# Reordering VectorE work in the opening of a fused attention and MLP kernel, with four softmax normalizations moved to GpSimd

## The chip, the core and the metric

The kernel runs on one core of a Trainium2 chip. The metric is the device time of one execution in microseconds. Engines are named as in the profile: PE is TensorE (matmul), PEld its weight loads, DVE is VectorE, ACT is ScalarE, POOL is GpSimd, SP is SyncE, which here only issues DMAs.

## The reference

Chunked attention, then two MLPs, all in float32 (the weights arrive as float64):

```python
scores = scale * np.matmul(q_c, k_c.transpose(0, 1, 2, 4, 3))     # chunks of 64
scores = scores - np.max(scores, axis=-1, keepdims=True)
attn = np.exp(scores)
attn = attn / (np.sum(attn, axis=-1, keepdims=True) + 1e-09)
out = np.matmul(attn, v_c)
...
h = x @ w_in                       # x: 2304 x 512, w_in: 512 x 2048
g = h * (1.0 / (1.0 + np.exp(-h)))
x = (g @ w_out)
...
a = x @ w_a                        # 512 x 1536
b = x @ w_b
return (a * b @ w_out).astype(np.float32)
```

## The kernel before

The 2304 tokens are 18 tiles of 128. A matrix product in full precision is made of three products of high and low parts: an operand is split by ACT, which writes a rounded high part, and by DVE, which subtracts it to leave the low part. That holds for the attention output (xhi, xlo), the activations (ghi, glo) and the weights (wA).

A weight tile of 128 x 512 passes six stations. SP fetches the float64 words into one of three slots of raws (`fetch`). ACT scales the upper words (`scaled`, L147). DVE makes the magnitude in two operations (`magnitude`, L155 and L158), then puts in sign and lower mantissa bits in two more (`begin`, L174 and L178). ACT rounds the high part (`upper`, L196). DVE subtracts for the low part (`lower`, L203). `weights` advances several tiles by one station in one call, and is called twice in each step of the first MLP. Tiles 0 and 1 of the weights are w_in[0] and w_out[0], tiles 2 and 3 w_in[1] and w_out[1], and so on; 32 of them pass L196 and L203.

The opening is written out by hand (source lines 816 to 902): it takes token tiles 0 to 5 through attention and mixes in the first weight tiles. For tile i, `S(i)` is the scores on PE (L253), `att_max` the row maximum and its subtraction on DVE (L267 to L272), `att_exp` the exponential on ACT, `att_norm` the sum, a reciprocal (L302) and a product with it (L303) on DVE, `Tr(i)` a transposition on PE (L312), `rest["P", i]` its copy out of PSUM by ACT (L316), `V(i)` the product with the values on PE (L335), `rest["X", i]` its high part by ACT (L347) and `rest["L", i]` its low part by DVE (L351). `V(4)` is written into the PSUM bank with the tag sA. `busy(n)` (L705) issues n idle matmuls on zeros, also into bank sA; each is two rows of the trace. Token tiles 0 to 3 are the first block of the MLP, tiles 4 and 5 a side block.

`front_a` is a product of the first MLP into bank mm or at (L370), followed on ACT by two sigmoid-gated activations (g at L399, ghi at L400) and on DVE by the low part glo (L396); `back` is the second product (L418). After the opening a loop over steps k follows: the next front product, the side block's back product, `weights`, the side block's front product, `weights`, the back product. Each engine takes its instructions in the order of the program; a PSUM bank or buffer that is reused makes its new writer wait for the last reader of the old contents.

Of the kernel before, what the change touches and what calls it, by code (L numbers as in the profile page):

```python
# [22 lines left out]
def chunk_attention_silu_mlp_gated_mlp(  # L23
# [35 lines left out]
    nc = tc.nc  # L59
# [43 lines left out]
    def bank(tag, shape):  # L103
        return psum.tile(shape, F32, tag=tag, name="ps_" + tag)

    def slot(name, dt=F32R):
        return big.tile([P, 4 * DM], dt, tag="b", name=name)
# [19 lines left out]
    def fetch(src, dest):  # L127
        raw = raws[:, turn[0] % RAWS]
        turn[0] += 1
        nc.sync.dma_start(out=raw, in_=src)  # L130
        fetched.append((dest, raw))

    def leave(n=0):

        while len(leaving) > n:
            dst, src = leaving.pop(0)
            nc.sync.dma_start(out=dst, in_=src)

    def words(raw):
        w32 = raw.bitcast(U32).rearrange("p (f t) -> p f t", t=2)  # L140
        return w32[:, :, 0], w32[:, :, 1]

    def scaled():

        dest, raw = fetched.pop(0)
        w = spool.tile([P, DM], F32, tag="tmp", name="w", bufs=3)
        nc.scalar.activation(w, words(raw)[1].bitcast(F32), AF.Copy, scale=2.0**111)  # L147
        opened.append((dest, raw, w))

    def magnitude():  # L150

        if not opened:
            return
        w = opened[0][2]
        nc.vector.tensor_scalar(  # L155
            out=w, in0=w, scalar1=2.0**-126, scalar2=2.0**-97, op0=ALU.mult, op1=ALU.mult
        )
        nc.vector.tensor_scalar(  # L158
            out=w.bitcast(U32),
            in0=w.bitcast(U32),  # L160
            scalar1=3,
            scalar2=0x7FFFFFFF,
            op0=ALU.logical_shift_left,
            op1=ALU.bitwise_and,
        )

    def begin():

        if not opened:
            return  # L170
        dest, raw, w = opened.pop(0)
        low, high = words(raw)
        wu = w.bitcast(U32)
        nc.vector.scalar_tensor_tensor(  # L174
            out=wu, in0=high, scalar=0x80000000, in1=wu,
            op0=ALU.bitwise_and, op1=ALU.bitwise_or,
        )
        nc.vector.scalar_tensor_tensor(  # L178
            out=wu, in0=low, scalar=29, in1=wu,
            op0=ALU.logical_shift_right, op1=ALU.bitwise_or,  # L180
        )
        if dest[0] == "f":
            wf[dest[1:]] = d = dram.tile([P, DM], F32, name=f"wf{dest[1]}{dest[2]}")
            leaving.append((d, w))
        else:
            stage_1.append((dest, w))

    def upper():
        if not stage_1:
            return  # L190
        dest, w = stage_1.pop()
        _, m, j = dest
        if m not in slots_a:
            slots_a[m] = slot("wA").rearrange("p (j n) -> p j n", j=4)
        hl = slots_a[m][:, 2 * j:2 * j + 2]
        nc.scalar.activation(hl[:, 0], w, AF.Copy)  # L196
        stage_2.append((dest, hl, w))

    def lower():
        if not stage_2:  # L200
            return
        dest, hl, w = stage_2.pop()
        nc.vector.tensor_tensor(out=hl[:, 1], in0=w, in1=hl[:, 0].bitcast(F32), op=ALU.subtract)  # L203
        wA.setdefault(dest[1], {})[dest[2]] = hl[:, 0], hl[:, 1]

    def weights(src, dest):

        leave()
        fetch(src, dest)
        upper()  # L210
        magnitude()
        begin()
        lower()
        scaled()


# [79 lines left out]
    def att_norm(i):  # L296
        s, mx, sm, rs, banks = soft[i]
        sg = s.rearrange("p h g k -> p g h k")
        if not banks:
            nc.vector.tensor_reduce(out=sm, in_=sg, op=ALU.add, axis=AX.X)  # L300
        nc.vector.tensor_scalar_add(sm, sm, EPS)
        nc.vector.reciprocal(out=rs, in_=sm)  # L302
        nc.vector.tensor_tensor(  # L303
            out=sg, in0=sg, in1=rs.unsqueeze(3).to_broadcast([P, 2, KT, 64]), op=ALU.mult
        )
        soft[i] = s

    def att_transpose(i, ptag, where, later=False):
        s = soft.pop(i).rearrange("p h g k -> p h (g k)")
        ps = bank(ptag, [P, KT, P])  # L310
        for hp in range(KT):
            nc.tensor.transpose(ps[:, hp, :], s[:, hp, :], ident)  # L312
        prob[i] = att_tile(where, "pt", i).rearrange("p (h n) -> p h n", h=KT)

        def evacuate():
            nc.scalar.activation(prob[i], ps, AF.Copy)  # L316

        if later:
            return evacuate
        evacuate()  # L320

    def att_values(i, ptags, x, o, later=False, beside=None):
        w = P // len(ptags)
        if beside is None:
            banks = [bank(t, [P, KT, w]) for t in ptags]
        else:
            banks = [t[:, 1 - r] for r, t in enumerate(soft[beside])]
        va = vs.pop(i).rearrange("p (a h d) -> p a h d", a=2, h=KT)
        half = [slice(0, 64), slice(64, 128)]
        for hp in range(KT):  # L330
            for a in range(2):
                for r in range(2):

                    ps, part, n = (banks[0], r, half[a]) if len(banks) == 1 else (banks[r], a, half[0])
                    nc.tensor.matmul(  # L335
                        ps[half[part], hp, n],
                        lhsT=va[half[r], a, hp, :],
                        rhs=prob[i][half[r], hp, half[a]],
                        start=True,
                        stop=True,  # L340
                    )
        parts = [[a[:, :, o + w * j:o + w * j + w] for a in x] for j in range(len(banks))]
        del prob[i]

        def upper():
            for ps, (hi, _) in zip(banks, parts):
                nc.scalar.activation(hi, ps, AF.Copy)  # L347

        def lower():
            for ps, (hi, lo) in zip(banks, parts):  # L350
                nc.vector.tensor_tensor(out=lo, in0=ps, in1=hi.bitcast(F32), op=ALU.subtract)  # L351

        if later:
            return upper, lower
        upper()
        lower()
# [288 lines left out]
    def next_a():  # L645
        m, j = units_a[done[0]]
        done[0] += 1
        return (w_in, w_out)[j][m], ("a", m, j)

    def prep_a():  # L650
        if done[0] < len(units_a):
            weights(*next_a())
            return True
        return False
# [8 lines left out]
    def prep_b():  # L663
        if done[1] < len(units_b):
            dest = units_b[done[1]]
            src = (w_a, w_b, w_o2)[dest[1]][dest[2]]
            weights(src, dest)
            done[1] += 1
            return True
        return False  # L670
# [11 lines left out]
    with tc.manual_schedule():  # L682
# [18 lines left out]
        def busy(n):  # L701

            ps = bank("sA", [P, P])
            for _ in range(n):
                nc.tensor.matmul(ps, lhsT=zero, rhs=zero, start=True, stop=True)  # L705

        def half(i):
            if blocks[0][1] > i:
                return x_t[0], i * P
            return x_t[SIDE], (i - blocks[0][1]) * P  # L710
# [9 lines left out]
        def v_in(*tiles):  # L720
            for i in tiles:
                load_v(i, W, nc.sync)
# [12 lines left out]
        qk_in(5)  # L735
        v_in(4)
        v_in(5)


        side_bank = {-1: "at", 0: "at", 1: "at"}  # L740

# [45 lines left out]
        def back(k):  # L787
            b, m = steps[k]
            back_a(b, m, pend.pop(k))
# [9 lines left out]
        def finish(g, k):  # L799
            if k in g:  # L800
                g[k][2]()
# [3 lines left out]
        rest = {}  # L805
# [4 lines left out]
        def Tr(i, tag):  # L810
            rest["P", i] = att_transpose(i, tag, W, later=True)

        def V(i, tag):
            rest["X", i], rest["L", i] = att_values(i, (tag,), *half(i), later=True)
# [10 lines left out]
        att_exp(1)  # L825
        magnitude()
        att_norm(0)
        busy(3)
        Tr(0, "at")
# [20 lines left out]
        rest["X", 1]()  # L850
        att_max(4, W, True)
        begin()
        fetch(*next_a())
        Tr(3, "sA")
        rest["P", 3]()
        rest["L", 1]()
# [22 lines left out]
        rest["X", 4]()  # L879
        pend[0], silu = front_a(main[0], 0, "mm", gpool, True)  # L880
        upper()
        Tr(5, "at")
        rest["L", 4]()
        lower()
        silu()
        rest["P", 5]()
        scaled()
        busy(2)
        V(5, "mm")
        finish(pend, 0)  # L890
        magnitude()
        begin()
        busy(2)
        back(0)
        rest["X", 5]()
# [430 lines left out]
```

## Time and profile before

| | |
|---|---|
| median of 3 runs | 863.2 us (862.88 to 863.54) |
| the profiled execution | 862.69 us, its span 860.9 us |
| PE busy | 846.5 us, 98% of the span |
| DVE busy | 566.7 us, 66% |
| ACT busy | 398.5 us, 46% |
| POOL busy | 50.2 us, 6% |
| PE in 0 to 30 us / 30 to 50 us | 24.14 us / 18.03 us busy |
| PE in 200 to 300 us | 100.00 of 100 us busy |
| granted TensorE clock, mean | 0.999 |

The span is the profiled time from the first to the last instruction; 1.8 us of the execution lie outside it. PE is the engine to watch: where it is busy throughout, other engines' work costs nothing; where it stands idle, the row of its next instruction says in brackets for how long and for whom.

### The profile page before, as it was taken

The page shows a single profiled execution, that of the slowest core. Times are in us where ns is not written, and L with a number is a line of the kernel's source. Part 1 is how long each engine was busy: PE and PEld are TensorE (multiplying, and loading weights), DVE is VectorE, ACT ScalarE, POOL GpSimd, SP SyncE. Part 2 cuts the span into 40 slices and gives each one's busy share as a digit, 9 for nine tenths or more (in the row PEclk, how much of TensorE's full clock was granted, in tenths as well). Part 3 has the DMA queues.
Part 4 walks back from the last instruction along what each step waited for, and adds up shares of the span by engine and source line. Part 5 has one row for each costly group of instructions (what it writes and reads, how often), then busy time and mean ns, then how long its engine had stood idle before and what let it go on. Part 6 is the DMA issues. An engine that isn't in the chain of part 4 may idle for free.

```text
span 860.9 us, 14124 instructions
## 1 busy us (share of the span) xinstructions
PE 846.5 (98%) x5474; PEld 769.5 (89%) x5474; DVE 566.7 (66%) x1029; ACT 398.5 (46%) x769; POOL 50.2 (6%) x91
## 2 busy tenths in 40 slices
PE   7999999999999999999999999999999999999998
PEld 7788888888888888888889999999999999999998
DVE  6886877855567755757865997584454594454563
ACT  5645546535454455434545554463333373333252
POOL 0000000010010100023201110000000000000000
PEclk9999999999999999999999999999999999999999
DMA  8354353337455654467799887878666888666761
GB/s 294 100 174 132 123 161 121 100 118 238 147 174 172 217 165 169 152 226 269 265 343 372 314 296 309 306 297 294 256 249 254 306 313 265 245 252 252 288 226 56
DMA packets 54034, 193.85 MB, mean 225 GB/s; under 512 B 5904, under 2 KB 13584, under 8 KB 45520
## 3 DMA queue, kind: packets, MB, share of 16 engines
q1 hardware_dynamic: 46752, 169.76, 55.5%
q0 software_dynamic: 6928, 22.81, 8.0%
q8 instruction: 43, 0.70, 0.3%
q10 hardware_dynamic: 288, 0.39, 0.1%
q14 instruction: 23, 0.19, 0.1%
HBM read 141.03 MB, written 51.90 MB: 224 GB/s over the span
## 4 chain that ended last, share of the span: by engine, by line
PE 86%; issue 5%; ACT 3%; DMA 3%; DVE 3%; POOL 0%; POOLq 0%; ACTq 0%; DVEq 0%
PE ps_acc L972 19%; PE ps_acc L418 19%; PE ps_mm L370 15%; PE ps_sA L370 7%; PE ps_at L972 5%; PE ps_sA L972 5%; PE ps_sB L972 4%; PE ps_mm L972 4%; DMA raws<-wf 2%; PE ps_sA L418 1%; PE ps_sB L418 1%; PE ps_at L370 1%; PE ps_at L253 1%; PE ps_at L335 1%; PE ps_sA L705 1%
## 5 line engine op out<-in xcount | busy, mean ns | idle before, releaser
L972 PE MATMUL ps_acc<-xo,ring 128*128 128x384 f32 x868 | 168.2, 334 | 0.6 <-DVE gq L1047 0.6
L418 PE MATMUL ps_acc<-ghi,wA 128*128 128x512 f32 x512 | 159.2, 392 | 0.0
L972 PEld LDWEIGHTS ps_acc<-xo,ring 128*128 128x128 f32 x868 | 152.1, 188 | 1.1 <-DVE gq L1047 1.1
L418 PEld LDWEIGHTS ps_acc<-ghi,wA 128*128 128x128 f32 x512 | 94.2, 188 | 19.1
L370 PE MATMUL ps_mm<-xhi,wA 128*128 128x512 f32 (+1 forms) x400 | 101.3, 375 | 3.2 <-ACT wA L196 3.2
L418 PE MATMUL ps_acc<-glo,wA 128*128 128x512 f32 x256 | 99.9, 390 | 0.0
L370 PEld LDWEIGHTS ps_mm<-xhi,wA 128*128 128x128 f32 x400 | 70.2, 188 | 17.3 <-ACT wA L196 5.1
L399 ACT ACTIVATE g<-ps_mm 128x512 f32<-128x512 f32 (+1 forms) x50 | 28.0, 559 | 102.5 <-PE ps_mm L370 96.3
L396 DVE TENSOR_TENSOR glo<-g,ghi 128x512 fp32r<-128x512 f32 x80 | 50.7, 633 | 27.2 <-ACT ghi L400 27.0
L418 PEld LDWEIGHTS ps_acc<-glo,wA 128*128 128x128 f32 x256 | 48.1, 188 | 10.2
L1107 DVE TENSOR_TENSOR u<-gq,u 128x384 fp32r<-128x384 f32 x84 | 44.5, 553 | 17.4 <-ACT u L1106 16.9
L1106 ACT ACTIVATE u<-gq 128x384 fp32r<-128x384 f32 x84 | 40.6, 516 | 30.5 <-DVE gq L1047 28.6
L972 PE MATMUL ps_acc<-u,ring 128*128 128x384 f32 x272 | 53.6, 337 | 0.3
L147 ACT ACTIVATE w<-raws 128x512 f32<-128x512 f32 x68 | 45.5, 670 | 16.6 <-DMA raws<-w_b 8.8
L370 PE MATMUL ps_mm<-xlo,wA 128*128 128x512 f32 (+1 forms) x200 | 49.9, 371 | 0.6 <-DVE xlo L351 0.6
L370 PE MATMUL ps_sA<-xhi,wA 128*128 128x512 f32 x184 | 49.6, 391 | 0.0
L972 PEld LDWEIGHTS ps_acc<-u,ring 128*128 128x128 f32 x272 | 47.6, 188 | 1.3 <-ACT gq L981 0.9
L178 DVE SCALAR_TENSOR_TENSOR w<-raws,w 128x512 uint32<-128x512 uint32 x68 | 47.1, 692 | 2.3
L174 DVE SCALAR_TENSOR_TENSOR w<-raws,w 128x512 uint32<-128x512 uint32 x68 | 47.1, 692 | 2.3
L972 PE MATMUL ps_at<-xo,ring 128*128 128x384 f32 x231 | 47.8, 334 | 0.0
L972 PE MATMUL ps_sB<-xo,ring 128*128 128x384 f32 x220 | 44.9, 334 | 0.0
L972 PE MATMUL ps_sA<-xo,ring 128*128 128x384 f32 x213 | 44.4, 335 | 0.1
(183 smaller groups left out, 1413.5 us busy)
## 6 DMA issues: line engine op xcount, KB each, us to landing
ring<-w SPq DMA_DIRECT2D x30, 1024.0 KB, 7.3
ring<-wg SPq DMA_DIRECT2D x24, 1024.0 KB, 5.1
ring<-wg SPq DMA_DIRECT2D x24, 768.0 KB, 6.3
wg<-ring SPq DMA_DIRECT2D x12, 1024.0 KB, 6.6
wf<-w SPq DMA_DIRECT2D x36, 256.0 KB, 2.2
wg<-ring SPq DMA_DIRECT2D x12, 768.0 KB, 6.5
raws<-w_in SPq DMA_DIRECT2D x16, 512.0 KB, 3.5
raws<-w_out SPq DMA_DIRECT2D x16, 512.0 KB, 3.5
```

The lines of the kernel that those rows point to most:

```text
L147: nc.scalar.activation(w, words(raw)[1].bitcast(F32), AF.Copy, scale=2.0**111)
L174: nc.vector.scalar_tensor_tensor(out=wu, in0=high, scalar=0x80000000, in1=wu, op0=ALU.bitwise_and, op1=ALU.bitwise_or,)
L178: nc.vector.scalar_tensor_tensor(out=wu, in0=low, scalar=29, in1=wu, op0=ALU.logical_shift_right, op1=ALU.bitwise_or,)
L253: nc.tensor.matmul(soft[i][j % len(soft[i])][n, j, hp, :], lhsT=q[r, hp, n], rhs=k[r, hp, n], start=True, stop=True,)
L335: nc.tensor.matmul(ps[half[part], hp, n], lhsT=va[half[r], a, hp, :], rhs=prob[i][half[r], hp, half[a]], start=True, stop=True,)
L370: nc.tensor.matmul(ps, lhsT=a[:, kk * P:(kk + 1) * P], rhs=b[:, kk, :], start=(j == 0 and kk == 0), stop=(j == 2 and kk == KT - 1),)
L396: nc.vector.tensor_tensor(out=glo, in0=g, in1=ghi.bitcast(F32), op=ALU.subtract)
L399: nc.scalar.activation(g, ps, AF.Silu)
L418: nc.tensor.matmul(acc_t[b][j], lhsT=a[:, j * P:(j + 1) * P], rhs=g, start=(m == 0 and i == 0 and (b != SIDE or j % 2 == 0)), stop=(m == M ...
L972: nc.tensor.matmul(ps, lhsT=a, rhs=b, start=first and i == 0, stop=last and i == 2, skip_group_check=True,)
L1106: nc.scalar.activation(hi, src, AF.Copy)
L1107: nc.vector.tensor_tensor(out=lo, in0=src, in1=hi.bitcast(F32), op=ALU.subtract)
```

## The change

There are four edits. In `weights`, `lower` moves ahead of `begin`. The fetch of weight tile 2 is written earlier. The L303 products of token tiles 2 to 5 go to GpSimd. Near the end of the opening, `scaled` and `magnitude` of weight tile 2 move up, and `rest["L", 4]`, the low part of token tile 4, moves down behind `begin`.

```diff
@@ weights
         upper()
         magnitude()
+        lower()
         begin()
-        lower()
         scaled()
@@ att_norm
-        nc.vector.tensor_tensor(
+        (nc.gpsimd if 1 < i < 6 else nc.vector).tensor_tensor(
             out=sg, in0=sg, in1=rs.unsqueeze(3).to_broadcast([P, 2, KT, 64]), op=ALU.mult
         )
@@ opening
         v_in(5)
-
+        fetch(*next_a())
...
         att_max(4, W, True)
         begin()
-        fetch(*next_a())
         Tr(3, "sA")
@@ opening
         pend[0], silu = front_a(main[0], 0, "mm", gpool, True)
         upper()
+        scaled()
         Tr(5, "at")
-        rest["L", 4]()
         lower()
         silu()
         rest["P", 5]()
-        scaled()
         busy(2)
         V(5, "mm")
+        magnitude()
         finish(pend, 0)
-        magnitude()
         begin()
+        rest["L", 4]()
         busy(2)
         back(0)
```

SP's rows and their order are the same in both kernels. DVE at the end of the opening, from the sum of token tile 5 on, before (`start` holds the probabilities, `ps_sA` is tile 4, `ps_mm` tile 5):

```order
L300 TENSOR_REDUCE sm<-start 128x8
L301 TENSOR_SCALAR sm<-sm 128x8
L302 RECIPROCAL rs<-sm 128x8
L303 TENSOR_TENSOR start<-start,rs 128x2x4x64
L351 TENSOR_TENSOR xlo<-ps_sA,xhi 128x4x128
L203 TENSOR_TENSOR wA<-w,wA 128x512
L396 TENSOR_TENSOR glo<-g,ghi 128x512
L155 TENSOR_SCALAR w<-w 128x512
L158 TENSOR_SCALAR w<-w 128x512
L174 SCALAR_TENSOR_TENSOR w<-raws,w 128x512
L178 SCALAR_TENSOR_TENSOR w<-raws,w 128x512
L351 TENSOR_TENSOR xlo<-ps_mm,xhi 128x4x128
```

and in the changed kernel:

```order
L300 TENSOR_REDUCE sm<-start 128x8
L301 TENSOR_SCALAR sm<-sm 128x8
L302 RECIPROCAL rs<-sm 128x8
L203 TENSOR_TENSOR wA<-w,wA 128x512
L155 TENSOR_SCALAR w<-w 128x512
L158 TENSOR_SCALAR w<-w 128x512
L396 TENSOR_TENSOR glo<-g,ghi 128x512
L174 SCALAR_TENSOR_TENSOR w<-raws,w 128x512
L178 SCALAR_TENSOR_TENSOR w<-raws,w 128x512
L351 TENSOR_TENSOR xlo<-ps_sA,xhi 128x4x128
L351 TENSOR_TENSOR xlo<-ps_mm,xhi 128x4x128
L203 TENSOR_TENSOR wA<-w,wA 128x512
```

The L303 row is gone from DVE, and the L351 row that reads ps_sA has moved behind L396, L174 and L178.

PE over the same stretch, with the semaphores that a row waits for, in the changed kernel (the rows are the first MLP product, Tr(5), busy(2) and V(5)):

```order
L370 MATMUL ps_mm<-xlo,wA 128x512 [waits DVE_49]
L370 MATMUL ps_mm<-xlo,wA 128x512 x3
L370 MATMUL ps_mm<-xhi,wA 128x512 x4
L312 MATMUL ps_at<-ident,start 128x128 [waits PE_49,Pool_49]
L312 MATMUL ps_at<-ident,start 128x128 x3
L705 MATMUL ps_sA<-start 128x128 [waits DVE_49]
L705 MATMUL ps_sA<-start 128x128
L335 MATMUL ps_mm<-start 64x64 [waits DMAHW3_49,Activation_49]
L335 MATMUL ps_mm<-start 64x64 x15
```

PE's rows stand in the same order as before; the transposition's wait has gone from DVE and ACT to POOL, and busy's first row waits for DVE in both kernels, since it writes the bank that the L351 row on ps_sA reads.

DVE in one call of `weights` in the loop and the glo behind it, before:

```order
L155 TENSOR_SCALAR w<-w 128x512
L158 TENSOR_SCALAR w<-w 128x512
L174 SCALAR_TENSOR_TENSOR w<-raws,w 128x512
L178 SCALAR_TENSOR_TENSOR w<-raws,w 128x512
L203 TENSOR_TENSOR wA<-w,wA 128x512
L396 TENSOR_TENSOR glo<-g,ghi 128x512
```

and in the changed kernel:

```order
L155 TENSOR_SCALAR w<-w 128x512
L158 TENSOR_SCALAR w<-w 128x512
L203 TENSOR_TENSOR wA<-w,wA 128x512
L174 SCALAR_TENSOR_TENSOR w<-raws,w 128x512
L178 SCALAR_TENSOR_TENSOR w<-raws,w 128x512
L396 TENSOR_TENSOR glo<-g,ghi 128x512
```

L203 now stands between the magnitude and the sign, in 27 calls.

## Rows read from the trace of the kernel before

**Rows 1.** Waits of PE over the span: us in total, times, longest
```profile
PE ps_mm L370 <- ACT wA L196: 3.2, 5, 1.3
```

**Rows 2.** PE in order of time: start, us, work, idle before
```profile
17.54 0.63 PE L312 MATMUL ps_sB<-ident,start 128*128 128x128 f32 x4 [0.52 <-DVE start L303]
...
29.01 1.20 PE L370 MATMUL ps_mm<-xlo,wA 128*128 128x512 f32 x4 [0.59 <-DVE xlo L351]
30.04 1.08 PE L370 MATMUL ps_mm<-xhi,wA 128*128 128x512 f32 x4
...
31.40 0.69 PE L705 MATMUL ps_sA<-start 128*128 128x128 f32 x4
32.79 1.15 PE L335 MATMUL ps_mm<-start 64*64 64x64 f32 x32 [0.70 <-ACT start L316]
33.87 0.71 PE L705 MATMUL ps_sA<-start 128*128 128x128 f32 x4
34.33 0.71 PE L418 MATMUL ps_acc<-ghi,wA 128*128 128x512 f32 x2
```

**Rows 3.** DVE in order of time, same stretch
```profile
16.70 0.69 DVE L303 TENSOR_TENSOR start<-start,rs 128x512 f32<-128x512 f32 x1
...
30.64 0.68 DVE L351 TENSOR_TENSOR xlo<-ps_sA,xhi 128x512 fp32r<-128x512 f32 x1
...
32.28 0.69 DVE L396 TENSOR_TENSOR glo<-g,ghi 128x512 fp32r<-128x512 f32 x1 [0.36 <-ACT ghi L400]
...
34.25 0.69 DVE L174 SCALAR_TENSOR_TENSOR w<-raws,w 128x512 uint32<-128x512 uint32 x1
34.97 0.69 DVE L178 SCALAR_TENSOR_TENSOR w<-raws,w 128x512 uint32<-128x512 uint32 x1
35.58 0.68 DVE L351 TENSOR_TENSOR xlo<-ps_mm,xhi 128x512 fp32r<-128x512 f32 x1
```

**Rows 4.** ACT in order of time, same stretch
```profile
28.54 1.28 ACT L399 ACT_TABLE_LOAD   x1
31.16 0.60 ACT L399 ACTIVATE g<-ps_mm 128x512 f32<-128x512 f32 x1 [1.34 <-PE ps_mm L370]
31.65 0.59 ACT L400 ACTIVATE ghi<-ps_mm 128x512 fp32r<-128x512 f32 x1
...
32.61 0.68 ACT L147 ACTIVATE w<-raws 128x512 f32<-128x512 f32 x1
```

**Rows 5.** POOL in order of time, its largest operation before the loop
```profile
1.02 0.29 POOL masks.py:199 TENSOR_SCALAR_AFFINE_SELECT ident<-ident 128x128 f32<-128x128 f32 x1
```

**Rows 6.** ACT, DVE, ACT and PE in order of time, first loop steps
```profile
42.60 0.63 ACT L196 ACTIVATE wA<-w 128x512 fp32r<-128x512 f32 x1
...
43.27 0.69 DVE L203 TENSOR_TENSOR wA<-w,wA 128x512 fp32r<-128x512 f32 x1 [1.09 <-ACT wA L196]
...
44.99 0.63 ACT L196 ACTIVATE wA<-w 128x512 fp32r<-128x512 f32 x1
...
45.68 1.20 PE L370 MATMUL ps_mm<-xhi,wA 128*128 128x512 f32 x4 [1.27 <-ACT wA L196]
```

**Rows 7.** DVE and ACT in order of time, softmax inside the loop
```profile
69.19 0.69 DVE L272 TENSOR_TENSOR s<-ps_at,mx 128x512 f32<-128x512 f32 x1
...
71.87 0.63 ACT L283 ACTIVATE s<-s 128x512 f32<-128x512 f32 x1
```

**Rows 8.** Busy us of PE, PEld, DVE, ACT, POOL in late stretches; PE clock
```profile
857.00:857.50 0.50, 0.33 (x2) 0.01 (x1) 0.00 (x0) 0.13 (x1) 0.00 (x0) 1.00 0.00 0
...
859.50:860.00 0.50, 0.00 (x0) 0.00 (x0) 0.00 (x0) 0.00 (x0) 0.00 (x0) 0.54 0.00 0
```

**Rows 9.** L705 in 0 to 7 and 7 to 40 us: ns min/median/max, starts
```profile
L705 PE MATMUL ps_sA<-start x24: 307/421/580, 1.1 to 6.2; 128*128 128x128 f32 x24
...
L705 PE MATMUL ps_sA<-start x38: 275/275/377, 7.5 to 34.3; 128*128 128x128 f32 x38
```

**Rows 10.** SP in order of time: the fetch of weight tile 2
```profile
13.91 0.33 SPq L130 DMA_DIRECT2D raws<-w_in  x1
```

## The prediction

> **What bounds the kernel now.** I read the busy times first, then PE's waits over the whole span, then PE, DVE and ACT in order of time through the opening. PE is busy almost throughout, so only what moves PE counts. Behind the opening PE's only repeated wait is for the high part of a weight tile, five times, 3.2 us in all [rows 1]. The opening is different: there PE stops for the others at every stage. It waits 0.52 us for a normalization before a transposition, 0.59 us for a low part inside the first product, and 0.70 us for a copy before V(5) at 32.79 [rows 2]. From V(5) on it works through to the wait before 45.68 [rows 2, 6]. So I ask one question of the opening: when does V(5) start? And one of the loop: does the wait before 45.68 grow?
>
> **The dear step: the moved low part of token tile 4.** Before, busy(2) starts at 31.40, just after DVE's subtraction on ps_sA ends (30.64 + 0.68 = 31.32) [rows 2, 3]. That is no accident: its first matmul overwrites the bank that the subtraction reads, and the rows of PE's order show it waiting for DVE in both kernels. The diff puts that subtraction behind glo, L174 and L178, but busy(2) stays where it is, ahead of V(5). PE takes its work in order, so V(5) and all behind it now wait for this chain:
>
> - the product's last four matmuls start at 30.04 and end at 31.12; g starts at 31.16, ghi 0.49 later, and ghi ends at 32.24; glo starts at 32.28 [rows 2 to 4];
> - glo lets the next DVE operation start 0.61 later (as L178 does L351, 34.97 to 35.58), L174 to L178 takes 0.72, L178 to L351 0.61 [rows 3]: the subtraction runs from 34.22 to 34.90;
> - busy(2) follows 0.08 later, as before, at 34.98, and what is behind it 0.46 after that (33.87 to 34.33) [rows 2]: V(5) at 35.44.
>
> Before it was 32.79, so this costs 2.65 us, if the product ends when it did. The copy for V(5) (0.6 us on ACT behind ghi) is long done. No work of PE's own fills the gap.
>
> **Normalization on GpSimd.** No tensor product on POOL is in the trace. Its nearest row is the affine select, 0.29 us for 128 columns [rows 5]; four times that for 512 columns is 1.16 us, which I take. Lower bound: DVE's own 0.69 us [rows 3]. Upper bound: 2.32 us, twice 1.16, for the second input. From DVE's L303 at 16.70 to the transposition at 17.54 are 0.84 us: 0.69 of work and 0.15 of handing over [rows 2, 3]. On POOL I add 0.08 us for the handing over from DVE, so the transposition slips by D + 0.15 + 0.08 - 0.84 = D - 0.61, or 0.55 us. The scores of tile 4 stand behind it on PE, DVE's maxima of tile 4 wait for them, and tile 4's own normalization adds another 0.55. Both slips reach the exponential's successors on ACT: 1.10 us at the table load. The table load ends at 29.82 and g starts at 31.16, a cover of 1.34 [rows 4]. The moved L147 takes 0.57 of that cover (0.68 less the 0.11 by which ACT's operations overlap, 31.16 to 31.65 against 0.60) [rows 4]. So g starts 1.10 + 0.57 - 1.34 = 0.33 us later, and the chain above with it. DVE's relief (0.61 us for each L303 it loses) is eaten by the first slip. With D = 0.69 the slips are nearly nothing and the relief remains: -0.53. With D = 2.32 the term is 3.42 + 0.57 - 1.34 = 2.65. Tile 5's product on POOL is hidden behind the long wait at busy(2).
>
> [...]
>
> **The low part ahead of the sign.** L203 needs ACT's L196 of the same call, and `begin` used to run while ACT got there. Now `begin` of the next tile stands behind that wait. At the first loop steps it matters: L196 of tile 3 runs from 42.60 to 43.23, L203 follows at 43.27 [rows 6]. Then L174 at 43.88 and L178 at 44.60, ending at 45.29; L196 of tile 4, which had run at 44.99, starts at 45.33. PE's product waits for exactly that [rows 6]: 0.34 us. Bounds: 0, if DVE catches up, and 0.34. Elsewhere there is room. The tightest other place that I found is the softmax inside the loop: its subtraction ends at 69.88; behind two more operations (0.72 + 0.61) it ends at 71.21, and the exponential starts at 71.87 in any case, behind its table load [rows 7]. That cover, 0.66 us, would have to go before four such places cost anything. The earlier L203 gains nothing, since PE's waits are for high parts [rows 1].
>
> **The fetch** is nothing: SP's order is unchanged, and the third tile was fetched at 13.91 already, long before ACT scales it [rows 10].
>
> **The clock.** Waiting in this way leaves PE silent from about 32.0, when Tr(5), some 0.6 us behind the product, is done, to 35.3: 3.3 us. The end of the trace shows what silence can do: PE's last work is in the half microsecond from 857.0, and in the one from 859.5 the granted clock has fallen from 1.00 to a mean of 0.54, on its way to the lower level, 1.2 GHz [rows 8]. So I expect a fall. Its price I take from the start: 24 rows of L705 took from 1.1 to past 6.2 us, some 0.22 each, at a median of 421 ns, against 275 ns later [rows 9] and 0.115 each from 33.87 to 34.33 [rows 2]. That stretch lost 24 x 0.1 = 2.4 us, my upper bound; the lower is 0. I take 1.4, somewhat over the middle, since long matmuls follow V(5). The Trainium skill (TensorE: Matmul & The Clock Gate, Part 1) states that idleness takes the clock to 1.2 GHz and work brings it back; by that the fall comes, and the traces so far bear it out at both ends.
>
> **The sum**: 2.65 + 0.33 + 0.34 + 1.4 = 4.7 us. On the profiled execution, 862.69 us (1.8 of it outside the span, untouched), that is 867.4; the median of the runs shown lies 0.5 higher, so 867.9 us.
>
> **The rivals.**
>
> 1. The wait comes, the clock stays up: 863.2 + 3.3 = 866.5 us. For it: an idle stretch of 1.27 us left the clock alone [rows 6]. Against: this one is longer than that at the end. It decides below the chosen sum, still slower.
> 2. GpSimd is the slow one, at or beyond the upper bound of 2.32: 2.65 + 2.65 + 0.34 + 1.4 = 7.0, or 870.2 us. For it: two inputs and a first use. Against: the affine select is no slower per column than half of that.
> 3. Not slower: busy(2)'s wait on DVE is met by an earlier operation than the moved subtraction. Then V(5) moves by the 0.33 of ACT alone and the loop by 0.34: 863.9 us. Against it: the start of busy(2) 0.08 us after that subtraction [rows 2, 3]. It decides if the wait is over by 32.5.
> 4. Faster: as 3, and the earlier weight work also ends all five waits for high parts: 863.9 - 3.2 = 860.7 us [rows 1]. Against it: the one before 45.68 ends with an L196 that stands behind ACT's activations, not behind DVE [rows 6].
>
> **How the numbers follow.** 0.62 for the wait with the fall of the clock, 0.23 for rival 1, 0.08 for rival 2, 0.05 for rival 3, 0.02 for rival 4. The wait with its bounds reaches from 2.65 - 0.53 = 2.1 us (no fall, cheap GpSimd, loop free) to past 6.5 (2.65 + 0.33 + 0.34 + 2.4 = 5.7, and 0.8 more for a GpSimd product of 1.56). The range is 865.4 to 869.8. It leaves out rivals 2 to 4 and the far tail. Within 0.2%, 1.7 us, a measurement of this kernel can hardly be told from no change: slower 0.92, the same 0.05, faster 0.03.
>
> **What would show it.** In the changed trace busy(2)'s row should carry an idle time of about 3 us put down to DVE's subtraction on ps_sA, with V(5) near 35.8, and the granted clock should dip to 0.5 within the next microseconds. The POOL rows give D; Tr(2) and Tr(4) give the slips. The product at 45.68 should come at about 49 plus the clock's loss, its wait about 0.3 longer. I am wrong if busy(2) starts right behind Tr(5), if the stall is there but a later stage takes it back, or if a POOL product takes several microseconds.

## The result and the profile after

The changed kernel takes 867.29 us in the median (865.42 to 869.07, six executions); the kernel before, on the same chip, 862.90 us (862.46 to 863.54). The ratio is 1.0052, with an interval of 1.0038 to 1.0066: slower by 4.4 us. The profiled execution is the shortest of the six, 865.42 us with a span of 863.7 us, against 862.69 us and 860.9 us before. The page gives its length, PE's busy time and POOL's:

```profile
span 863.7 us, 14132 instructions
...
PE 846.5 (98%) x5474; PEld 769.4 (89%) x5474; DVE 562.4 (65%) x1025; ACT 399.0 (46%) x769; POOL 54.5 (6%) x95
```

PE is busy for the same 846.5 us as before, so the loss has to be found as waits. PE's waits over the span (us in total, times, longest) have one new entry of 3.0 us, and the one for high parts has grown:

```profile
PE ps_mm L370 <- ACT wA L196: 3.5, 5, 1.6
PE ps_sA L705 <- DVE xlo L351: 3.0, 1, 3.0
```

The second line did not exist before; the first was 3.2 us, longest 1.3 [rows 1]. Smaller changes are that the transpositions of tiles 2, 4 and 5 now wait for POOL, and that the waits of 0.59 and 0.70 us [rows 2] are gone. Now PE in order of time (start, us, work, idle before), to be read against [rows 2, 6]:

```profile
17.84 0.66 PE L312 MATMUL ps_sB<-ident,start 128*128 128x128 f32 x4 [0.89 <-POOL start L303]
...
25.42 0.65 PE L312 MATMUL ps_at<-ident,start 128*128 128x128 f32 x4 [1.05 <-POOL start L303]
...
29.06 1.09 PE L370 MATMUL ps_mm<-xlo,wA 128*128 128x512 f32 x4
...
31.32 0.65 PE L312 MATMUL ps_at<-ident,start 128*128 128x128 f32 x4 [0.25 <-POOL start L303]
34.97 0.71 PE L705 MATMUL ps_sA<-start 128*128 128x128 f32 x4 [3.00 <-DVE xlo L351]
35.61 1.15 PE L335 MATMUL ps_mm<-start 64*64 64x64 f32 x32
...
39.99 0.66 PE L370 MATMUL ps_at<-xhi,wA 128*128 128x256 f32 x4
...
48.83 1.19 PE L370 MATMUL ps_mm<-xhi,wA 128*128 128x512 f32 x4 [1.59 <-ACT wA L196]
```

Before busy(2) at 34.97, PE stands idle for 3.00 us, and V(5) starts at 35.61 instead of 32.79. The product of the loop comes at 48.83 instead of 45.68, its own wait 1.59 instead of 1.27 us. The transposition of tile 4, at 25.42 here, had this row before:

```profile
24.64 0.63 PE L312 MATMUL ps_at<-ident,start 128*128 128x128 f32 x4 [0.60 <-DVE start L303]
```

DVE in the same stretch shows what PE waits for:

```profile
29.72 0.64 DVE L203 TENSOR_TENSOR wA<-w,wA 128x512 fp32r<-128x512 f32 x1
30.28 1.27 DVE L155 TENSOR_SCALAR w<-w 128x512 f32<-128x512 f32 x1
31.58 0.43 DVE L158 TENSOR_SCALAR w<-w 128x512 uint32<-128x512 uint32 x1
32.29 0.69 DVE L396 TENSOR_TENSOR glo<-g,ghi 128x512 fp32r<-128x512 f32 x1 [0.29 <-ACT ghi L400]
32.90 0.68 DVE L174 SCALAR_TENSOR_TENSOR w<-raws,w 128x512 uint32<-128x512 uint32 x1
33.62 0.69 DVE L178 SCALAR_TENSOR_TENSOR w<-raws,w 128x512 uint32<-128x512 uint32 x1
34.23 0.68 DVE L351 TENSOR_TENSOR xlo<-ps_sA,xhi 128x512 fp32r<-128x512 f32 x1
```

The subtraction that ended at 31.32 before [rows 3] now ends at 34.23 + 0.68 = 34.91, behind glo, L174 and L178, and busy(2) follows 0.06 us later. ACT's rows, beside [rows 4], show that the product, and with it g, is not to blame; the last one is the high part that the loop's product waits for:

```profile
29.21 0.66 ACT L147 ACTIVATE w<-raws 128x512 f32<-128x512 f32 x1
29.88 1.28 ACT L399 ACT_TABLE_LOAD   x1
31.17 0.60 ACT L399 ACTIVATE g<-ps_mm 128x512 f32<-128x512 f32 x1
...
48.15 0.63 ACT L196 ACTIVATE wA<-w 128x512 fp32r<-128x512 f32 x1 [0.21 <-DVE w L178]
```

g starts at 31.17, before at 31.16, now directly behind its table load. POOL has the four normalizations: the first three take 1.04 us each, the last one 1.31:

```profile
16.74 1.04 POOL L303 TENSOR_TENSOR start<-start,rs 128x512 f32<-128x512 f32 x1 [15.43 <-ACT start L283]
...
29.95 1.31 POOL L303 TENSOR_TENSOR start<-start,rs 128x512 f32<-128x512 f32 x1 [4.59 <-ACT w L147]
```

The granted clock did not fall in this execution, neither in the silence nor behind it. The stretches below give from:to, length, busy time of PE and its instructions, granted clock (the 1.00 behind the bracket), and share and GB/s of the DMA:

```profile
32.00:33.00 1.00, 0.00 (x0) 1.00 0.00 0
...
35.00:36.00 1.00, 1.00 (x16) 1.00 0.53 106
```

### The profile page after: what moved, and what is told of

The parts are those of the page before. It is cut to its first block, busy times and chain, and to the rows that moved or that the text cites. A ratio compares the mean times of both kernels' runs of the same rounds, so it can differ in the third digit from the quotient of the medians.

```text
span 863.7 us, 14132 instructions
## 1 busy us (share of the span) xinstructions
PE 846.5 (98%) x5474; PEld 769.4 (89%) x5474; DVE 562.4 (65%) x1025; ACT 399.0 (46%) x769; POOL 54.5 (6%) x95
## 4 chain that ended last, share of the span: by engine, by line
PE 84%; issue 6%; ACT 3%; DVE 3%; DMA 2%; POOL 0%; ACTq 0%; POOLq 0%; DVEq 0%
PE ps_acc L418 19%; PE ps_acc L971 19%; PE ps_mm L370 14%; PE ps_sA L370 7%; PE ps_at L971 5%; PE ps_sA L971 5%; PE ps_sB L971 4%; PE ps_mm L971 4%; DMA raws<-wf 2%; PE ps_sA L418 1%; PE ps_at L370 1%; PE ps_sB L418 1%; PE ps_at L335 1%; PE ps_sA L705 1%; PE ps_at L253 1%
## 5 line engine op out<-in xcount | busy, mean ns | idle before, releaser
L971 PE MATMUL ps_acc<-xo,ring 128*128 128x384 f32 x868 | 168.2, 334 | 0.3 <-DVE gq L1046 0.3
L971 PEld LDWEIGHTS ps_acc<-xo,ring 128*128 128x128 f32 x868 | 152.0, 188 | 0.7 <-DVE gq L1046 0.7
L396 DVE TENSOR_TENSOR glo<-g,ghi 128x512 fp32r<-128x512 f32 x80 | 50.7, 633 | 29.9 <-ACT ghi L400 29.7
L971 PE MATMUL ps_acc<-u,ring 128*128 128x384 f32 x272 | 53.6, 337 | 0.3
L147 ACT ACTIVATE w<-raws 128x512 f32<-128x512 f32 x68 | 45.5, 671 | 15.5 <-DMA raws<-w_b 9.2
L971 PEld LDWEIGHTS ps_acc<-u,ring 128*128 128x128 f32 x272 | 47.6, 188 | 1.3 <-ACT gq L980 0.8
L178 DVE SCALAR_TENSOR_TENSOR w<-raws,w 128x512 uint32<-128x512 uint32 x68 | 47.1, 692 | 2.3
L971 PE MATMUL ps_at<-xo,ring 128*128 128x384 f32 x231 | 47.8, 334 | 0.0
L174 DVE SCALAR_TENSOR_TENSOR w<-raws,w 128x512 uint32<-128x512 uint32 x68 | 46.9, 689 | 1.3
L971 PE MATMUL ps_sB<-xo,ring 128*128 128x384 f32 x220 | 44.9, 334 | 0.0
L971 PE MATMUL ps_sA<-xo,ring 128*128 128x384 f32 x213 | 44.4, 335 | 0.1
```

Of the source, the lines that this page charges most:

```text
L174: nc.vector.scalar_tensor_tensor(out=wu, in0=high, scalar=0x80000000, in1=wu, op0=ALU.bitwise_and, op1=ALU.bitwise_or,)
L178: nc.vector.scalar_tensor_tensor(out=wu, in0=low, scalar=29, in1=wu, op0=ALU.logical_shift_right, op1=ALU.bitwise_or,)
L396: nc.vector.tensor_tensor(out=glo, in0=g, in1=ghi.bitcast(F32), op=ALU.subtract)
L971: nc.tensor.matmul(ps, lhsT=a, rhs=b, start=first and i == 0, stop=last and i == 2, skip_group_check=True,)
```

## The experiments

Theory: the moved subtraction makes busy(2) wait for the bank it reads, and that is most of the loss; GpSimd and the order inside the weight calls cost some tenths each; the rest is the clock. Rivals: GpSimd's products, or the new order of the weight work, are what delays V(5). Times stand beside the kernel before on the same chip: 862.62 us for the first four, 862.72 for the next three and 862.86 for the last three.

A place is compared between traces by its distance from ACT's exponential of tile 2 (L283), since executions differ by some tenths at their start. Its row before, and then in the changed kernel:

```profile
16.07 0.68 ACT L283 ACTIVATE start<-start 128x512 f32<-128x512 f32 x1
```

```profile
15.98 0.68 ACT L283 ACTIVATE start<-start 128x512 f32<-128x512 f32 x1
```

V(5) comes 32.79 - 16.07 = 16.72 us behind it before, and 35.61 - 15.98 = 19.63 after: 2.91 later. The product of the loop: 29.61 before, 32.85 after, 3.24 later.

**The subtraction put back, all else changed.**

```diff
+        rest["L", 4]()
         lower()
 ...
         begin()
-        rest["L", 4]()
         busy(2)
```

> The changed kernel with the low part of token tile 4 back in its old place, all else of the change kept. If the wait for the bank of tile 4 is the cost (theory): busy(2) no longer waits, V(5) starts near 32.8 us instead of 35.6, the wait before the loop's second main product stays at about 1.6, the clock stays up, and the time is that of the kernel before plus 0.3, about 863.2 us. If the slower transpositions behind GpSimd were the cost (rival 1): V(5) stays near 35 and the time near 867. If L203 ahead of the sign were (rival 2): the time stays 2 us or more above the kernel before, with the loss behind 46 us.

Measured: 863.21 us, ratio 1.0005 (0.9996 to 1.0013), 0.6 us over the kernel before. The wait at busy(2) is gone, V(5) is 0.32 us later than before and the loop's product 0.66. Of both, 0.2 us is not the change's: in this execution V(1), behind the transposition of tile 2, takes 0.2 us longer than in the changed kernel's trace, where PE has the same work at that place. The moved line carries nearly all of the loss.

**The subtraction left where the change puts it, busy(2) in another bank.**

```diff
-        def busy(n):
+        def busy(n, tag="sA"):
 ...
-            ps = bank("sA", [P, P])
+            ps = bank(tag, [P, P])
 ...
-        busy(2)
+        busy(2, "sB")
```

(The last pair stands twice, for the two calls around V(5).)

> The changed kernel as it is, the low part of tile 4 late, but the last two rounds of idle matmuls write bank sB instead of sA. Theory: it is only the shared bank that makes PE wait, so V(5) starts near 32.8 us and the time is about 863.2 us, as when the subtraction is moved back. Rival: what counts is DVE's order (the late subtraction is needed by someone else, or weight tile 2 takes DVE's time), then V(5) or the side block's first product is late by 1 to 3 us and the time stays above 865.

Measured: 863.10 us, ratio 1.0004 (0.9995 to 1.0013). PE in order of time:

```profile
31.71 0.61 PE L705 MATMUL ps_sB<-start 128*128 128x128 f32 x4
32.70 1.15 PE L335 MATMUL ps_mm<-start 64*64 64x64 f32 x32 [0.38 <-ACT start L316]
```

V(5) is 0.09 us later than before. The late low part by itself costs PE nothing: it ended at 34.81 in this trace, long behind V(5)'s start at 32.70, and PE did not wait for it. What costs is that a filler matmul, whose result nobody reads, overwrites the bank that the subtraction still reads. Against the changed kernel, V(5) is 2.82 us sooner by the other bank alone.

**The silence filled, the wait kept.**

```diff
+        busy(13, "sB")
         busy(2)
         V(5, "mm")
```

(busy with the bank as its argument, as above; it adds 13 filler matmuls, 26 rows of the trace.)

> The changed kernel with 13 more idle matmuls (26 rows of 0.115 us, 3.0 us) in bank sB ahead of those in sA, so that PE works through the time in which it waits for the subtraction. The wait itself ends when it did. Theory: the stall costs 2.7 us by itself and the fall of the clock, in most executions, another 1 to 4; with the silence filled every execution has a granted clock of 0.999, the spread falls below 0.8 us and the median is 862.9 + 2.7 = 865.6 us. Rival: the spread of the changed kernel has another cause, then clock and spread stay as they were (865.4 to 869.1), median about 867.3.

Measured: 865.59 us (865.12 to 866.82, five executions), ratio 1.0035 (1.0023 to 1.0048). PE works from 32.33 to 35.40, and V(5) and the loop's product stand where they stand in the changed kernel, 19.62 and 32.84 us behind the exponential. The profiled execution takes 865.50 us, as long as that of the changed kernel, 865.42, in which the clock did not fall behind the wait: filled or silent, the wait costs the same. The median is 3.0 us over the kernel before, where the traces' shift at the loop is 3.2; the changed kernel's is 4.4. The difference of 1.4 us is what I had put down to the clock, but the intervals of the two ratios overlap, the spread of 1.7 us is wider than the 0.8 expected, and the mean granted clocks are 0.997 to 1.000, not 0.999 throughout. By the times alone this speaks for the clock and doesn't settle it. The mean clocks of all executions on record say more: 0.996 or less stands in four of the six of the changed kernel and in three of the five of the next run, the two kernels in which PE is silent for 3 us or more, and in none of the other 168 that the experiments timed.

**The subtraction moved, nothing else changed.**

```diff
-        rest["L", 4]()
         lower()
 ...
         begin()
+        rest["L", 4]()
         busy(2)
```

> The kernel before with one edit: the low part of tile 4 moved behind the sign of weight tile 2, nothing else. There magnitude comes after glo and waits for ACT's scaling, so the subtraction comes later than in the changed kernel: L178 ends near 35.66 as before, the subtraction near 36.3, V(5) at 36.8, 4.0 us late. Theory: with the clock's part 863 + 4.0 + 1 to 2 = 868 to 869 us, slower than the whole change. Rival: if GpSimd or the loop carry the loss, this edit alone costs less than 1 us, 863 to 864.

Measured: 869.08 us, ratio 1.0076 (1.0063 to 1.0089). PE waits 4.75 us and V(5) starts 4.92 us later than before, where 4.0 were expected. Of the 4.92, 0.67 come from ahead of the edit: in this execution PE stands still inside V(1), 13 us before the edit's place, and the first product is already late by that much. The edit's part is 4.25. Here the clock did fall behind the wait in the profiled execution. PE in order of time, then windows as above:

```profile
19.18 0.97 PE L335 MATMUL ps_acc<-start 64*64 64x64 f32 x26 [0.37 <-issue]
...
37.37 0.81 PE L705 MATMUL ps_sA<-start 128*128 128x128 f32 x4 [4.75 <-DVE xlo L351]
38.10 1.97 PE L335 MATMUL ps_mm<-start 64*64 64x64 f32 x32
40.01 1.22 PE L705 MATMUL ps_sA<-start 128*128 128x128 f32 x4
40.88 0.88 PE L418 MATMUL ps_acc<-ghi,wA 128*128 128x512 f32 x2
...
43.87 0.66 PE L370 MATMUL ps_at<-xhi,wA 128*128 128x256 f32 x4
```

```profile
37.00:37.50 0.50, 0.13 (x1) 1.00 0.00 0
37.50:38.00 0.50, 0.50 (x4) 0.85 0.98 131
38.00:39.00 1.00, 1.00 (x17) 0.50 0.64 238
...
41.00:41.50 0.50, 0.50 (x4) 0.73 0.00 0
41.50:42.00 0.50, 0.50 (x4) 1.00 0.00 0
```

V(5) takes 1.97 instead of 1.15 us at the lower level, 1.2 GHz. From the start of V(5) to the next product are 43.87 - 38.10 = 5.77 us; before it was 37.17 - 32.79 = 4.38, and in the changed kernel's trace 39.99 - 35.61 = 4.38 as well. The row of before is:

```profile
37.17 0.66 PE L370 MATMUL ps_at<-xhi,wA 128*128 128x256 f32 x4
```

One fall costs 1.39 us here. With the 4.92 that is 6.3; the profiled execution is 6.7 us longer than that of before, of which 0.4 lie ahead of the exponential, and the median 6.5. The changed kernel's delay is 2.0 us shorter. Of this, 0.67 is the halt in V(1), and 1.3 come from the weight work ahead of the moved subtraction, which starts sooner there: L155 runs at 30.28, ahead of glo, behind an L147 that stands ahead of the table load. Here L147 stands behind ghi and the copy for V(5), and L155 runs only behind glo, as DVE's rows of this kernel show:

```profile
34.37 0.43 DVE L155 TENSOR_SCALAR w<-w 128x512 f32<-128x512 f32 x1 [0.34 <-ACT w L147]
...
36.63 0.68 DVE L351 TENSOR_TENSOR xlo<-ps_sA,xhi 128x512 fp32r<-128x512 f32 x1
```

**The order inside the weight calls alone.**

```diff
-        begin()
         lower()
+        begin()
         scaled()
```

> The kernel before with the low-part subtraction ahead of the sign in every call, nothing else. Theory: the second main product starts 0.3 us later (near 46.0 instead of 45.7), since L196 of weight tile 4 waits for DVE's sign; all other waits stay, and the time is 863.2 us, not to be told from 862.9. Rival: DVE runs late at the four softmax places of the loop (their waits of 0.48 grow to 1 or more each): 865 or more. Other rival: the low parts were late before, and some waits shrink: 862 or less.

Measured: 862.97 us, ratio 1.0003 (0.9994 to 1.0012). V(5) doesn't move, and the loop's wait is that of the changed kernel:

```profile
46.10 1.20 PE L370 MATMUL ps_mm<-xhi,wA 128*128 128x512 f32 x4 [1.59 <-ACT wA L196]
```

The trace shows the 0.3 us (1.59 against 1.27, the product 0.31 later); the times agree with it and cannot tell it from nothing.

**GpSimd alone, for tiles 2 to 5.**

```diff
-        nc.vector.tensor_tensor(
+        (nc.gpsimd if 1 < i < 6 else nc.vector).tensor_tensor(
```

> The kernel before with the products of token tiles 2 to 5 on GpSimd, nothing else. Theory: the transpositions of tiles 2 and 4 start 0.3 and 0.8 us later, DVE's low part of tile 3 comes 0.3 earlier, and the two cancel at the end of the first product; V(5) at 32.8 within 0.3; time 862.9 within 0.4. Rival: GpSimd's product is held up by DVE's operations on two SBUF inputs, tile 5 comes 1 us or more late and V(5) with it: 864 or more.

Measured: 863.01 us, ratio 1.0005 (0.9995 to 1.0014); V(5) 0.21 us later. In this execution too V(1) takes 0.2 us longer, 1.28 against 1.08 in the changed kernel's trace, so GpSimd's own part is about nothing:

```profile
18.49 1.28 PE L335 MATMUL ps_acc<-start 64*64 64x64 f32 x29
```

This small sum hides a loss and a gain, which four more kernels took apart, each with another condition in that one line:

- `2 < i < 6`:

> The kernel before with the products of tiles 3 to 5 alone on GpSimd; tile 2, whose transposition PE waits for, stays on DVE. Theory: no slip at tile 2, 0.4 at tile 4 (1.04 on GpSimd against 0.69), and DVE's low part of tile 3 comes 0.6 us earlier, so that the first product ends 0.3 us earlier than before and V(5) starts near 32.5: 862.6 us, too little to be told from 862.9 by the clock on the wall, but the trace should show it. Rival: PE's transposition of tile 4 bounds the product, then V(5) is at 32.8 or later.

- `2 < i < 6`, once more:

> The same kernel as before with GpSimd for tiles 3 to 5, run once more. Theory (the gain in its trace is real: V(5) 0.44 us sooner after tile 3's exponential than before, since the product no longer waits 0.59 us for its low part and the copy's wait falls from 0.70 to 0.48): 0.4 to 0.6 us below the kernel before, an interval below 1. Rival (the 0.5 us of the first run were scatter): within 0.2 us of it.

- `3 < i < 6`:

> The kernel before with GpSimd for tiles 4 and 5 alone. Theory (tile 3's normalization has slack on either engine, and what gains is that DVE loses tile 4's ahead of the low parts): the same as with tiles 3 to 5, 0.4 to 0.6 us below the kernel before, no wait for a low part in the first product. Rival (DVE's relief at tile 3 is what lets it catch up): the wait of 0.59 us is back and the time is that of the kernel before.

- `i in (3, 5)`:

> The kernel before with GpSimd for tiles 3 and 5, tile 4 again on DVE. Theory (tile 4's place is what counts): the product waits some 0.6 us for its low part as before, V(5) as before, time within 0.2 us of the kernel before. Rival (tile 3's or tile 5's relief carries the gain): 0.4 to 0.6 us below it.

| tiles on GpSimd | time, us | ratio and interval | V(5) against before, us |
|---|---|---|---|
| 2 to 5 | 863.01 | 1.0005 (0.9995 to 1.0014) | +0.21 |
| 3 to 5 | 862.18 | 0.9993 (0.9984 to 1.0002) | -0.44 |
| 3 to 5, again | 862.36 | 0.9996 (0.9987 to 1.0005) | -0.48 |
| 4 and 5 | 862.39 | 0.9994 (0.9985 to 1.0003) | -0.45 |
| 3 and 5 | 862.76 | 1.0000 (0.9991 to 1.0009) | +0.01 |

V(1) takes its usual time in the last four. Tile 2 is the loss: PE has nothing to do while it waits for that normalization, and of the 0.65 us between the first two rows all but V(1)'s 0.2 are due to it. Tile 4 is the gain, as the first product shows in the kernel with tiles 4 and 5 on GpSimd, and then in the one with 3 and 5:

```profile
25.17 0.66 PE L312 MATMUL ps_at<-ident,start 128*128 128x128 f32 x4 [0.98 <-POOL start L303]
...
28.81 1.09 PE L370 MATMUL ps_mm<-xlo,wA 128*128 128x512 f32 x4
```

```profile
24.74 0.63 PE L312 MATMUL ps_at<-ident,start 128*128 128x128 f32 x4 [0.62 <-DVE start L303]
...
29.10 1.19 PE L370 MATMUL ps_mm<-xlo,wA 128*128 128x512 f32 x4 [0.60 <-DVE xlo L351]
```

With tile 4 on GpSimd its transposition waits 0.4 us longer, but DVE comes to the low part sooner, and the wait of 0.60 us in the product is gone. The product then ends 0.4 us sooner, and V(5), which waits for the copy behind ghi, starts sooner. The best kernel of the study, GpSimd for tiles 3 to 5 or 4 and 5, is some 0.5 us below the kernel before in each of three comparisons, two of them with the same runs of the kernel before. Each interval reaches 1, where the repeated run was expected to stay below it, so by the times alone the gain is not shown; the traces show V(5) sooner each time.

## Why the prediction was right

867.9 us was forecast and 867.29 measured, inside the range, on the side that held 0.92. The steps one by one:

- **The dear step, 2.65 us.** Right, and for the reason given. The chain was forecast as glo 32.28, subtraction 34.22 to 34.90, busy(2) 34.98; the rows read 32.29, 34.23 to 34.91 and 34.97. (This execution's exponential comes 0.09 us sooner, so measured from there all of them are 0.1 later, which is the GpSimd step below.) Only the last step was short: from busy(2) to V(5) it is 0.64 us, not 0.46. The bank alone is worth 2.82 us (the run with the other bank). The run with the subtraction put back gives 19.63 - 17.04 = 2.59, and 2.8 without the 0.2 us that its V(1) lost.
- **GpSimd, 0.33 us.** Right in kind, too large: 0.10. A product takes 1.04 us, not 1.16, so the transpositions slip by 0.39 and 0.87 - 0.39 = 0.48 us, not 0.55 each. The table load is 13.90 us behind the exponential instead of 12.47: 1.43 later, of which the cover of 1.34 takes all but 0.09. That is where g stands (15.19 against 15.09). The Trainium skill (GPSIMD Engine Reference, 3.1 Elementwise) gives 4497 ns for a `tensor_tensor` addition of 2048 float32 columns; a quarter of it, 1.12 us, is an estimate by that page for this product. The trace's 1.04 is nearer to that than to the 1.16 scaled from the affine select. What this step had wrong is that DVE's relief "is eaten by the first slip": tile 4's relief is worth more than tile 4's slip, as the last runs show.
- **The low part ahead of the sign, 0.34 us.** Right: 0.31 in the trace of the run that changes this alone, 0.32 in the wait of the changed kernel. The mechanism is the forecast one: L196 at 48.15 waits for DVE's L178, which `lower` had pushed back. The loop pays it once: the five waits for high parts grow by 0.3 us in all.
- **The fetch, nothing.** No row speaks against it, but it was not tried by itself. Nor were the moved `scaled` and `magnitude`; the run with the subtraction moved alone bears on them, since without them the wait is longer.
- **The clock, 1.4 us.** This is the weakest step. The fall that the changed kernel's trace was to show did not come: the clock stayed at 1.00, and the time was 865.42 us. That execution is rival 1, the wait without the fall. The other five took 1.5 to 3.7 us more, at mean granted clocks of 0.994 to 0.997 against 0.999, so a fall in them is likely; where it lies stays open, since they left no trace. The size agrees with 1.39 us in the run with the subtraction moved alone. That it agrees so closely is luck, for 1.4 was a choice between 0 and 2.4. Its source was sound: four L705 rows at 1.2 GHz take 0.22 us each in that run (40.01 to 40.88), as the 24 rows of the start did, although the granted clock in the trace of before reads 1.00 there.
- **The sum.** 2.91 for V(5), 0.33 more at the loop's product and 1.4 for the clock are 4.6 us; the medians differ by 4.4. The spans of the two profiled executions, in neither of which the clock fell in the opening, differ by 2.8: of the 3.24 at the loop's product 0.35 is won back at 528 us, where a wait for DVE in the second MLP (L971) is 0.26 instead of 0.61, and 0.09 is the earlier start.
- **The rivals.** GpSimd as the slow one falls with 1.04 us a product. "Not slower" is close to what the kernel would have been without the shared bank: 0.5 us over the kernel before, where that rival had 0.7. "Faster" falls too, since all five waits for high parts are still there.

## What to carry to other kernels

Before moving an operation later, ask who next writes the memory that it reads: its consumers may have time to spare while a filler, whose result nobody needs, stands next in the queue of the bottleneck engine and waits for the bank. Here a second bank for the filler took the wait away, and the order of the rest did not have to change. When work is given to a slower engine, decide tile by tile: set the time by which the bottleneck gets that tile later against the time by which the old engine's next work comes sooner. Here tile 2 only lost, tile 4 gained more than it lost, and the sum of both reads as nothing. And before two traces are compared at a late place, look whether they already differ ahead of the edit.

## What the runs showed of the hardware

**DVE and GpSimd hold each other up.** In the changed kernel L203 on DVE, two inputs from SBUF, starts at 29.72; the product that POOL starts at 29.95 takes 1.31 us instead of 1.04; and L155 on DVE, 0.42 us elsewhere, takes 1.27 and ends 0.29 us behind POOL. In the run with GpSimd alone it is L203 that is held, 1.26 us instead of 0.68, while a subtraction from a PSUM bank that runs into the start of POOL's product takes its usual time. DVE and POOL in order of time:

```profile
30.03 0.64 DVE L351 TENSOR_TENSOR xlo<-ps_sA,xhi 128x512 fp32r<-128x512 f32 x1
30.58 1.26 DVE L203 TENSOR_TENSOR wA<-w,wA 128x512 fp32r<-128x512 f32 x1
```

```profile
30.25 1.04 POOL L303 TENSOR_TENSOR start<-start,rs 128x512 f32<-128x512 f32 x1 [4.61 <-DVE rs L302]
```

The Trainium skill (SBUF — State Buffer, SBUF: two separate sides) states that a DVE operation with two SBUF inputs, or in a two-port performance mode, and a GpSimd operation share a pair of ports as an exclusive lock: the one that starts first keeps it for its whole instruction, and the other one blocks. The rows of L203 and POOL agree: each time the later one ends behind the earlier by nearly its own usual time (0.90 of 1.04 us for POOL at 29.95, 0.55 of 0.68 for L203 at 30.58). L155 behaves in the same way, 0.29 of 0.42; in which mode it runs, no row shows. Here the hold cost nothing: L155's 0.85 us lie before ghi, which glo waits for.

**How long PE was idle does not by itself tell whether the clock falls.** In the run with the subtraction moved alone, the granted clock still read 1.00 from 36.00 to 37.50, at the end of 4.75 us of waiting, and fell only when PE had started again at 37.37. It was back at 1.00 by 41.5. The 3.00 us of the changed kernel left it at 1.00 in its profiled execution. At the end of the trace of before it fell in the silence itself, over 2 us behind PE's last work [rows 8]. And there is an earlier place: near 11 us, where PE waits for k of a token tile. In the run with the filled wait it waited 1.99 us there, to 11.21, and from 13.00 on the clock was at 0.50:

```profile
15.00:16.00 1.00, 1.00 (x25) 0.50 1.02 385
16.00:17.00 1.00, 1.00 (x14) 0.86 1.03 381
```

The same fall stands in both traces with GpSimd for tiles 3 to 5, behind waits of 1.75 and 2.50 us, and not in the trace with the other bank, behind 2.62. It costs little there: the two executions took 862.00 and 862.81 us, where that kernel's medians are 862.18 and 862.36. What decides between these cases, no run here shows.
